# Asking for the first expert weights earlier and casting them later, in a fused attention and mixture-of-experts kernel

## The chip, the core and the metric

The kernel runs on one core of one Trainium2 chip. Five engines work side by side, each through its own list of instructions in order: TensorE (PE, with its weight loads as PEld), VectorE (DVE), ScalarE (ACT), GpSimd (POOL) and SyncE (SP), which here only issues transfers. They wait for each other through semaphores. The metric is the device time in microseconds (us), the median of several runs.

## The reference

```
a    = softmax(phi)                       # [8, 8, 576, 32], over the last axis
k_m  = a^T k ;  v_m = a^T v               # 32 memory slots for each batch and head
attn = softmax(q k_m^T / 8) ;  x = attn v_m   # -> 4608 tokens x 512
e    = argmax(x w_gate)                   # one expert of 8 for each token
gate = softmax(x w_gate)[e] * sigmoid(x w_output_gate)[e]
out  = gate * (relu(x w1[e]) w2[e])       # w1 512 x 1024, w2 1024 x 512
```

## The kernel before

**Two parts share the engines.** The attention goes through 20 groups, five for each of four pairs of batches. The memory part (`memory`) sums k and v into 32 slots per head; `scores`, `shift`, `expo`, `divide`, `back` and `values` make a group's attention; ACT copies the result out of PSUM (`xo`, line 902) and SP stores it to DRAM (`xs<-xo`, lines 1011 and 1015). After each pair `rank` and `route_early` or `route_late` sort its tokens by expert. The second part runs tokens of one expert through w1 and w2 in up to 36 slots; each slot gathers its tokens from `xs` (`xg`) and takes eight weight tiles of 512 KB (`w<-wall`, line 563).

**The order is written out by hand.** In each turn `t` the words of the list `ORDER` are gone through: S is `shift` of group t, X `expo` of group t-1, V0 and V1 the two halves of `values` of group t-3 with their copies, C `scores` of group t+1, M and m a step of the memory part, R a step of the routing, W the weights (`LAG` holds these distances). In turn 17 (`START`), after word S, the program opens: from there the slots' matmuls are the main stream, and three words of the attention are put in after each dozen or half dozen of them (`HOOK`). So what stands before the opening is attention alone, and what stands after it is matmuls of the experts with attention in between.

**Weights.** `Stream.fetch` issues loads while a raw buffer is free (three before the opening, two more after it, `raw`). `Stream.split` makes the pair of tiles `whl` that the matmuls use: ACT casts the raw tile to the rounded type (line 574) and DVE subtracts the cast from the raw tile (line 588). `take` and `done` call it, and word W calls it twice in turn 16, so that two tiles are ready at the opening. The loads of the first three tiles are issued by word W in turn 14.

**What can hold what.** SP issues transfers in the order of the program. The tile `xo` has two buffers, one for each turn: the copies of a turn wait until the store of the turn two before has landed. The tile `qt` has three; word C asks for the q of the group three ahead. `loads` asks for k and v in pairs of tiles, one pair for each step of `sums`. `pr` is one PSUM tile that the routing's small matmuls take in turn: `take_pr` waits in the program's order until the holder has issued its last read, `hold` lets a number of words pass, and only semaphores keep the next matmul from overtaking that read on the chip. After the opening the matmuls write `bps`, four PSUM banks in turn; the gathered tokens are first turned by PE (line 1086), then cast by ACT to `xh` (line 1088) and subtracted by DVE to `xl` (line 1089), then w1 follows (line 1238) and w2 (line 1275).

Of the kernel before, what the change touches and what calls it, by code (L numbers as in the profile page):

```python
# [18 lines left out]
B, H, S, D, M = 8, 8, 576, 64, 32  # L19
NTOK, DM, E, F = 4608, 512, 8, 1024  # L20
NBP = B // 2
# [13 lines left out]
NSLOT = NPE + NPT + NPP + NSS  # L35
NTHR = 13

ORDER = ["R4", "W", "X", "S", "R0", "m", "D", "M", "B", "V0", "R1", "R1", "V1", "M", "m", "C"]
LAG = {"X": 1, "B": 2, "D": 1, "V": 3, "C": -1}
TICK = 0  # L40
HOOK = (3, 2)
# [27 lines left out]
def attention_moe(tc, phiT, kv, qT, wgo, wall, out):  # L69
# [3 lines left out]
    with contextlib.ExitStack() as ctx:  # L73
# [206 lines left out]
        def route_early(k):  # L280
# [2 lines left out]
            eo, en = epcs[k], epcs[k + 1]  # L283
            yield from hold(LATE["ct"])
            yield from take_pr()
            n_ = counts(AFTER[k])
            yield
            yield from hold(LATE["dve"])
# [389 lines left out]
        def loads():  # L678

            load_phi(0)  # L680
            for bp in range(NBP):
                for c in (0, 2, 4, 6):
                    load_kv(bp, c)
                    load_kv(bp, c + 1)
                    if bp == 0 and c == 2:
                        load_kv(0, 8)
                        load_q(0)
                        load_q(1)
                    if bp == 0 and c == PHI1:
                        load_phi(1)  # L690
                    if bp == 0 and c == 6:
                        for n in range(2, NQ):
                            load_q(n)
                    yield

        def soften(bp):
# [414 lines left out]
        def attention():  # L1111

            nonlocal rou
            st, lgs = {}, {}
            while 0 not in kTs:
                mem.step()
            st[0] = scores(0, 0)
# [2 lines left out]
            for t in range(NT + LAG["V"]):  # L1120
                for w in ORDER:
                    g = t - LAG.get(w[0], 0)
                    if w in ("M", "m"):
                        if w == "M" or t % 5 < 4:
                            mem.step()
                    elif w[0] == "R":

                        if len(left) < NBP - 1:
                            rou.step(int(w[1:]) * (2 if len(left) == 1 else 1))
                    elif w == "W":  # L1130

                        if t == START - 3:
                            stream.fetch()
                        while t == START - 1 and stream.split(2):
                            pass
                    elif w == "V0" and 0 <= g < NT:
                        bp, c = g // 5, g % 5
                        while 2 * bp + (c >= 2) not in ves:
                            mem.step()
                        if g == 5 * bp:  # L1140
                            lgs[bp] = rt.tile([P, NCH, 16], F32, name="lg", bufs=2)
                        xo = wk.tile([P, 2, 2, 2 * XQ], F32, name="xo", bufs=2)
                        values(bp, 2 * c, st[g], xo)
                    elif w == "V1" and 0 <= g < NT:
                        if c < 4:
                            values(bp, 2 * c + 1, st[g], xo)
                        store(bp, c, xo, lgs[bp])
                    elif w == "C" and 0 < g < NT:
                        while 2 * (g // 5) + (g % 5 >= 2) not in kTs:
                            mem.step()  # L1150
                        st[g] = scores(g // 5, g % 5)
                        if g + NQ < NT:
                            load_q(g + NQ)
                    elif w == "S" and 0 <= g < NT:
                        shift(st[g])
                    elif w == "X" and 0 <= g < NT:
                        expo(st[g])
                    elif w == "D" and 0 <= g < NT:
                        divide(st[g])
                    elif w == "B" and 0 <= g < NT:  # L1160
                        back(st[g])
# [282 lines left out]
```

## Time and profile before

| | |
|---|---|
| runs | 553.48, 555.34, 555.79 us; median 555.34 |
| the profiled execution | 555.06 us, span 553.2 us |
| PE busy | 509.3 us, 92% of the span |
| ACT, DVE, POOL busy | 288.4, 351.1, 233.0 us |
| mean granted TensorE clock | 0.967 |
| first expert matmul (line 1238) | 119.32 us |
| transfers | 123.54 MB, mean 223 GB/s |

The profile is of one execution. Times count from the first instruction. The span is the time from the first to the last instruction; the run's own time has 1.9 us more around it. The granted clock is a share of full speed: 1.00 is 2.4 GHz and 0.50 is 1.2 GHz. "Idle before" names what ended an engine's idle time; where a wait is for several things, the profile puts it down to the one that came last, which is not always the one that held it.

### The profile page before, as it was taken

How to read it: one execution, taken by the hardware profiler on the slowest of the kernel's cores; microseconds unless marked ns; L12 is line 12 of the kernel's file. 1: busy time of each engine (PE TensorE's matmuls, PEld its weight loads, DVE VectorE, ACT ScalarE, POOL GpSimd, SP SyncE). 2: the span in 40 equal slices, each digit the busy share in tenths (PEclk: the TensorE clock that was granted, in tenths of full speed). 3: DMA queues.
4: the chain of work that ended last, by engine and by line, in shares of the span. 5: the costliest groups of instructions: out<-in, count | busy, mean ns of one | idle time of the engine just before them, and what ended most of it. 6: DMA issues, size and time to landing. Idle time of an engine off the chain costs nothing. (4 is left out here: it accounts for less than half of the span.)

```text
span 553.2 us, 10563 instructions
## 1 busy us (share of the span) xinstructions
PE 509.3 (92%) x3850; PEld 438.6 (79%) x3850; DVE 351.1 (63%) x779; ACT 288.4 (52%) x536; POOL 233.0 (42%) x254
## 2 busy tenths in 40 slices
PE   3778697779999999999999999999999999999993
PEld 2454465469689889898898989898999899988982
DVE  4274987677875649997555564954695387729310
ACT  3475565555345455643444554854685386548310
POOL 2242576750444223510376471745366453721101
PEclk9977978979999999999999999999999999999997
DMA  8999999995556846964456574776586578643001
GB/s 297 418 390 390 407 333 364 368 371 171 152 182 193 271 135 232 323 189 143 144 162 223 152 240 129 247 229 228 154 259 194 202 221 254 207 162 103 30 21 43
DMA packets 41998, 123.54 MB, mean 223 GB/s; under 512 B 10256, under 2 KB 10320, under 8 KB 41552
## 3 DMA queue, kind: packets, MB, share of 16 engines
q1 hardware_dynamic: 35136, 102.71, 56.3%
q0 software_dynamic: 6800, 20.06, 10.2%
q8 instruction: 32, 0.52, 0.4%
q14 instruction: 30, 0.25, 0.2%
HBM read 102.40 MB, written 20.35 MB: 222 GB/s over the span
## 5 line engine op out<-in xcount | busy, mean ns | idle before, releaser
L1275 PE MATMUL bps<-whl,hh 128*128 128x512 f32 x640 | 193.1, 394 | 0.0
L1238 PE MATMUL bps<-xh,whl 128*128 128x384 f32 x640 | 166.0, 336 | 0.7 <-DVE xl L1089 0.7
L588 DVE TENSOR_TENSOR whl<-w,whl 128x1024 fp32r<-128x1024 f32 x112 | 136.3, 1221 | 15.5 <-ACT whl L574 15.4
L1275 PEld LDWEIGHTS bps<-whl,hh 128*128 128x128 f32 x640 | 119.9, 188 | 24.6 <-issue 0.2
L574 ACT CAST whl<-w 128x1024 fp32r<-128x1024 f32 x112 | 116.6, 1045 | 22.1 <-PE bps L1275 16.3
L1238 PEld LDWEIGHTS bps<-xh,whl 128*128 128x128 f32 x640 | 115.8, 188 | 2.1 <-DVE xl L1089 0.9
L529 POOL DMA_INDIRECT xg<-xs,idx_ql x84 | 99.9, 1189 | 25.6 <-issue 23.5
L1238 PE MATMUL bps<-xl,whl 128*128 128x384 f32 x320 | 107.0, 334 | 0.0
L1275 PE MATMUL bps<-whl,hl 128*128 128x512 f32 x240 | 93.7, 390 | 0.0
L1243 DVE SCALAR_TENSOR_TENSOR hl<-bps,hh 128x384 fp32r<-128x384 f32 x80 | 44.0, 555 | 61.4 <-ACT hh L1242 61.4
L1242 ACT ACTIVATE hh<-bps 128x384 fp32r<-128x384 f32 x80 | 38.9, 492 | 77.7 <-PE bps L1238 77.6
L1211 POOL DMA_INDIRECT out<-y,idx_ol x23 | 24.9, 1084 | 108.7 <-ACT y L1210 52.4
L1238 PEld LDWEIGHTS bps<-xl,whl 128*128 128x128 f32 x320 | 60.1, 188 | 0.3
L1275 PEld LDWEIGHTS bps<-whl,hl 128*128 128x128 f32 x240 | 45.1, 188 | 8.5
L869 POOL TENSOR_TENSOR ea<-ea,mx 128x512 f32<-128x512 f32 (+1 forms) x20 | 19.2, 962 | 50.4 <-DVE mx L867 46.0
L1233 PE MATMUL bps<-xh,whl 128*128 128x384 f32 x128 | 37.7, 338 | 0.0
L1234 PE MATMUL bps<-xh,whl 128*128 128x256 f32 x128 | 35.7, 279 | 0.0
L902 ACT COPY xo<-bpd 128x576 f32<-128x576 f32 x36 | 22.7, 639 | 22.6 <-issue 9.0
L1210 ACT ACTIVATE y<-bps,gx 128x512 f32<-128x512 f32 x19 | 13.1, 688 | 40.1 <-PE bps L1275 28.6
L1211 POOL DMA_INDIRECT out<-y,idx_ob x9 | 9.8, 1087 | 49.4 <-ACT y L1210 37.4
L900 PE MATMUL bpd<-ve_b,aT 64*128 64x144 f32 (+1 forms) x320 | 29.0, 333 | 0.7 <-DVE ea L863 0.5
L863 DVE STREAM_TRANSPOSE ea<-bpd 128x512 f32<-128x512 f32 (+1 forms) x20 | 13.2, 659 | 25.0 <-PE bpd L853 25.0
(263 smaller groups left out, 599.0 us busy)
## 6 DMA issues: line engine op xcount, KB each, us to landing
w<-wall SPq DMA_DIRECT2D x112, 512.0 KB, 4.6
kvt<-kv SPq DMA_DIRECT2D x32, 512.0 KB, 8.3
xs<-xo SPq DMA_DIRECT2D x16, 576.0 KB, 5.8
qt<-qT SPq DMA_DIRECT2D x16, 512.0 KB, 9.3
ph<-phiT SPq DMA_DIRECT2D x3, 1152.0 KB, 11.9
kv<-kv SPq DMA_DIRECT2D x4, 512.0 KB, 9.2
xg<-xs,idx_ql POOLq DMA_INDIRECT x84, 4.5
ph<-phiT SPq DMA_DIRECT2D x4, 288.0 KB, 3.8
```

The costliest lines, as they stand in the source:

```text
L529: G.indirect_dma_start(out=z["xg"][:, k, XQ * b:XQ * b + XQ], out_offset=None, in_=xs[0:z["rows"]].rearrange("t (a q) -> (t a) q", a=4), i ...
L574: A.copy(hl[:, 0], w[:])
L588: V.tensor_tensor(hl[:, 1], w[:], hl[:, 0].bitcast(F32), ALU.subtract)
L900: T.matmul(px[to:to + n, r, sl], z["aT"][h, o:o + n], ves[2 * bp + b][h, g], start=True, stop=True)
L902: A.copy(xo[:, c % 2], px[:, :, 0:2 * XQ])
L1211: G.indirect_dma_start(out=out, out_offset=bass.IndirectOffsetOnAxis(ap=z["idx"][1][0:n, z["q0"] + k:z["q0"] + k + 1], axis=0), in_=y[0:n] ...
L1233: T.matmul(pb, w[:, 0, o:o + P], x[0][:, cc], start=(cc == 0), stop=False)
L1234: T.matmul(pb[:, 0:256], w[:, 1, o:o + P], x[0][:, cc, 0:256], start=False, stop=(cc == 3))
L1238: T.matmul(pb, w[:, b, o:o + P], x[a][:, cc, 0:n_], start=(n == 0), stop=(n == 11))
L1242: A.activation(h_[:, j], pb, AF.Relu)
L1243: V.scalar_tensor_tensor(l_[:, j], pb, 0.0, h_[:, j].bitcast(F32), ALU.max, ALU.subtract)
L1275: T.matmul(py[k], a, w[:, b, DM * f:DM * f + DM], start=(u == 4 and f == 0 and n == 0), stop=(u == 7 and f == 1 and n == len(ps) - 1))
```

## The change

It has three parts. The first three weight loads leave word W of turn 14 and go into `loads`, right behind the last k and v; word W moves from ahead of X to behind V1, so that the two casts of turn 16 stand behind the copies of that turn. The q of groups 18 and 19 is no longer asked for by word C of turns 14 and 15, but by word X of turn 17, just ahead of the opening. The second call of `route_early` lets three more words pass before its count matmul (line 277).

```diff
-ORDER = ["R4", "W", "X", "S", "R0", "m", "D", "M", "B", "V0", "R1", "R1", "V1", "M", "m", "C"]
+ORDER = ["R4", "X", "S", "R0", "m", "D", "M", "B", "V0", "R1", "R1", "V1", "W", "M", "m", "C"]
...
             yield from take_pr()
+            if k:
+                yield from hold(LATE["pe"])
             n_ = counts(AFTER[k])
...
                         for n in range(2, NQ):
                             load_q(n)
+                    if (bp, c) == (NBP - 1, 6):
+                        stream.fetch()
                     yield
...
-            st, lgs = {}, {}
+            st, lgs, held = {}, {}, []
...
                     elif w == "W":
 
-                        if t == START - 3:
-                            stream.fetch()
                         while t == START - 1 and stream.split(2):
                             pass
...
-                        if g + NQ < NT:
+                        if START < g + NQ < NT:
+                            held.append(g + NQ)
+                        elif g + NQ < NT:
                             load_q(g + NQ)
...
                     elif w == "X" and 0 <= g < NT:
+                        while t == START and held:
+                            load_q(held.pop(0))
                         expo(st[g])
```

**SP's queue, from the last k and v to the opening.** `w` are weights, `kvt` k and v, `qt` q, `xo` the copies of the attention's result and `gt` the gates of a pair. The stores of turns 13 to 16 are those of `xo_1526`, `xo_1628`, `xo_1729`, `xo_1805` before, and `xo_1541`, `xo_1628`, `xo_1727`, `xo_1791` now. Before:

```order
L675 DMA kvt_1515<-kv 128x1024
L675 DMA kvt_1517<-kv 128x1024
L1011 DMA xs_60<-xo_1526 128x2x576
L670 DMA qt_1582<-qT 128x1024
...
L563 DMA w_1610<-wall 128x1024
...
L563 DMA w_1612<-wall 128x1024
...
L563 DMA w_1614<-wall 128x1024
L1011 DMA xs_60<-xo_1628 128x2x576
L670 DMA qt_1681<-qT 128x1024
```

and now:

```order
L677 DMA kvt_1515<-kv 128x1024
L677 DMA kvt_1517<-kv 128x1024
...
L565 DMA w_1528<-wall 128x1024
...
L565 DMA w_1530<-wall 128x1024
...
L565 DMA w_1532<-wall 128x1024
L1015 DMA xs_60<-xo_1541 128x2x576
L672 DMA qt_1597<-qT 128x1024
L1015 DMA xs_60<-xo_1628 128x2x576
```

Three weights now stand ahead of the store of turn 13 and of the q of group 17. Further down, the fourth and fifth weight come behind the store of turn 16, and the two late q behind these.

**ACT, the last instructions ahead of the opening,** with what each waits for (`DMAHW` are semaphores of SP's transfers). `xo_1729` before and `xo_1727` now are the copies of turn 15. Before:

```order
L902 COPY xo_1729<-bpd_1730 128x576 [waits DMAHW5_49,DVE_49,PE_49]
L902 COPY xo_1729<-bpd_1736 128x576 [waits PE_49]
L574 CAST whl_1771<-w_1610 128x1024 [waits DMAHW7_49]
L574 CAST whl_1776<-w_1612 128x1024 [waits DMAHW0_49]
L873 ACTIVATE ea0_203<-ea0_203 128x16x32 [waits Pool_49]
L779 ACTIVATE kvm_1787<-pk_1647,rs_1338 128x128 [waits PE_49]
...
L902 COPY xo_1805<-bpd_1806 128x576 [waits DMAHW2_49,DVE_49,PE_49]
L902 COPY xo_1805<-bpd_1812 128x576 [waits PE_49]
L873 ACTIVATE ea1_204<-ea1_204 128x16x32 [waits Pool_49]
L1088 CAST xh_1876<-bps_1878 128x384 [waits PE_49]
```

and now:

```order
L906 COPY xo_1727<-bpd_1728 128x576 [waits DMAHW0_49,DVE_49,PE_49]
L906 COPY xo_1727<-bpd_1734 128x576 [waits PE_49]
L877 ACTIVATE ea0_203<-ea0_203 128x16x32 [waits Pool_49]
L783 ACTIVATE kvm_1773<-pk_1647,rs_1338 128x128 [waits PE_49]
...
L906 COPY xo_1791<-bpd_1792 128x576 [waits DMAHW2_49,DVE_49,PE_49]
L906 COPY xo_1791<-bpd_1798 128x576 [waits PE_49]
L576 CAST whl_1805<-w_1528 128x1024 [waits DMAHW5_49]
L576 CAST whl_1810<-w_1530 128x1024 [waits DMAHW6_49]
L877 ACTIVATE ea1_204<-ea1_204 128x16x32 [waits Pool_49]
L1092 CAST xh_1876<-bps_1878 128x384 [waits PE_49]
```

The two casts move from behind the copies of turn 15 to behind those of turn 16. DVE's two subtractions move with them: they now stand directly ahead of these rows, which before followed on turn 16's own work:

```order
L590 TENSOR_TENSOR whl_1805<-w_1528,whl_1805 128x1024 [waits DMAHW5_49,Activation_49]
L590 TENSOR_TENSOR whl_1810<-w_1530,whl_1810 128x1024 [waits DMAHW6_49,Activation_49]
L811 COPY ve_b_1774<-bpa_1815 128x2x16 [waits PE_49]
L867 STREAM_TRANSPOSE ea2_205<-bpd_1825 128x16x32 [waits DVE_49,PE_49]
L871 TENSOR_REDUCE mx_1850<-ea2_205 128x16 [waits DVE_49]
L1023 TENSOR_REDUCE lg_1540<-xo_1791 128x32
L1093 TENSOR_TENSOR xl_1877<-bps_1878,xh_1876 128x384 [waits Activation_49]
```

**PE, the count matmul of the second `route_early`** (line 277 in both). Before:

```order
L1086 MATMUL bps<-ident,xg 128x128 x3
L1275 MATMUL bps<-whl,hh 128x512
L1275 MATMUL bps<-whl,hl 128x512
L1275 MATMUL bps<-whl,hh 128x512 x2
L1275 MATMUL bps<-whl,hl 128x512
L1275 MATMUL bps<-whl,hh 128x512
L277 LDWEIGHTS ones_b
L277 MATMUL pr<-ohc_91,ones_b 128x8
```

and now:

```order
L1090 MATMUL bps<-ident,xg 128x128 x3
L1281 MATMUL bps<-whl,hh 128x512
L1281 MATMUL bps<-whl,hl 128x512
L1281 MATMUL bps<-whl,hh 128x512 x2
L1281 MATMUL bps<-whl,hl 128x512
L1281 MATMUL bps<-whl,hh 128x512 x2
L1281 MATMUL bps<-whl,hl 128x512
L1281 MATMUL bps<-whl,hh 128x512 x2
L1281 MATMUL bps<-whl,hl 128x512
L1281 MATMUL bps<-whl,hh 128x512
L277 LDWEIGHTS ones_b
L277 MATMUL pr<-ohc_91,ones_b 128x8
```

Six matmuls of 512 columns more stand ahead of it.

## Rows read from the trace of the kernel before

**Rows 1.** Who waited for whom on PE from 118 us to the end: engine, line, what it waited for; us in total, times, longest us. These are all rows of the answer.

```profile
PE pr L277 <- DVE w__2038 L963: 1.0, 1, 1.0
PE bps L1238 <- DVE xl L1089: 0.7, 1, 0.7
```

**Rows 2.** The timeline of PE around the opening: start us, us, engine, line, operation, tiles, count, and in brackets the idle time before and what ended it.

```profile
104.40 1.25 PE L900 MATMUL bpd<-ve_b,aT 64*128 64x144 f32 x16
...
107.65 0.67 PE L853 MATMUL bpd<-qt,kT 64*32 64x256 f32 x16 [0.78 <-ACT xo L902]
112.79 0.74 PE L788 MATMUL bpa<-ident,kvm 128*128 128x128 f32 x2 [4.47 <-ACT kvm L779]
113.45 2.29 PE L900 MATMUL bpd<-ve_b,aT 64*128 64x144 f32 x16
...
116.90 1.77 PE L1086 MATMUL bps<-ident,xg 128*128 128x128 f32 x12
119.32 0.45 PE L1238 MATMUL bps<-xh,whl 128*128 128x384 f32 x1 [0.65 <-DVE xl L1089]
...
128.74 0.66 PE L853 MATMUL bpd<-qt,kT 64*32 64x256 f32 x16
```

**Rows 3.** The timeline of ACT around the opening, columns as in Rows 2.

```profile
106.96 1.18 ACT L902 COPY xo<-bpd 128x576 f32<-128x576 f32 x2 [3.19 <-PE pk L768]
109.39 1.04 ACT L574 CAST whl<-w 128x1024 fp32r<-128x1024 f32 x1 [1.25 <-DMA w<-wall]
110.90 1.04 ACT L574 CAST whl<-w 128x1024 fp32r<-128x1024 f32 x1 [0.47 <-DMA w<-wall]
111.85 0.63 ACT L873 ACTIVATE ea<-ea 128x512 f32<-128x512 f32 x1
112.38 0.61 ACT L779 ACTIVATE kvm<-pk,rs 128x128 f32<-128x128 f32 x2
...
115.79 0.64 ACT L902 COPY xo<-bpd 128x576 f32<-128x576 f32 x1 [0.32 <-PE bpd L900]
116.33 0.63 ACT L873 ACTIVATE ea<-ea 128x512 f32<-128x512 f32 x1
```

**Rows 4.** The timeline of SP's queue ahead of the opening (start us, us of issuing, line, transfer, count). The row at 106.88 is the second store of `gt`, which waits for the store of the row at 97.58 to land.

```profile
97.58 0.38 SPq L1011 DMA_DIRECT2D xs<-xo  x1
...
100.16 1.68 SPq L563 DMA_DIRECT2D w<-wall  x3
...
106.88 0.96 SPq L983 DMA_DIRECT2D xs<-gt  x1
108.11 0.38 SPq L980 DMA_DIRECT2D xs<-gt  x1
...
113.73 1.64 SPq L563 DMA_DIRECT2D w<-wall  x2
```

**Rows 5.** What SP's queue waited for from 80 to 130 us: us in total, times, longest us.

```profile
SPq L983 <- DMA xs<-xo: 1.0, 1, 1.0
SPq L983 <- DMA w<-wall: 0.9, 1, 0.9
```

**Rows 6.** The timeline of POOL: the subtraction of group 15's row maximum, which `expo` in turn 16 waits for.

```profile
108.32 1.04 POOL L869 TENSOR_TENSOR ea<-ea,mx 128x512 f32<-128x512 f32 x1
```

**Rows 7.** The timeline of DVE around the opening, columns as in Rows 2.

```profile
110.47 1.23 DVE L588 TENSOR_TENSOR whl<-w,whl 128x1024 fp32r<-128x1024 f32 x1 [3.76 <-ACT whl L574]
...
116.16 0.19 DVE L807 COPY ve_b<-bpa 128x32 f32<-128x32 f32 x1
117.08 0.72 DVE L863 STREAM_TRANSPOSE ea<-bpd 128x512 f32<-128x512 f32 x1 [0.74 <-PE bpd L853]
...
118.72 1.94 DVE L1089 TENSOR_TENSOR xl<-bps,xh 128x384 fp32r<-128x384 f32 x4
...
125.27 2.36 DVE L588 TENSOR_TENSOR whl<-w,whl 128x1024 fp32r<-128x1024 f32 x2 [0.38 <-ACT whl L574]
```

**Rows 8.** The timeline of PE around the count matmul of the second `route_early`.

```profile
144.71 0.40 PE L1275 MATMUL bps<-whl,hh 128*128 128x512 f32 x1
146.10 0.18 PE L277 MATMUL pr<-ohc,ones_b 128*128 128x8 bf16 x1 [1.00 <-DVE w__2038 L963]
146.15 0.48 PE L1275 MATMUL bps<-whl,hh 128*128 128x512 f32 x1
...
147.39 0.62 PE L1275 MATMUL bps<-whl,hh 128*128 128x512 f32 x2
```

**Rows 9.** The timeline of DVE: the last read of `pr` ahead of that matmul.

```profile
145.83 0.22 DVE L963 TENSOR_TENSOR w__2038<-ohg,pr 128x72 f32<-128x72 bf16 x1
```

**Rows 10.** The timeline of PE: two more places in the attention where PE had stood still.

```profile
63.80 0.17 PE L277 MATMUL pr<-ohc,ones_b 128*128 128x8 bf16 x1 [2.03 <-DVE ohc L944]
...
85.72 0.59 PE L788 MATMUL bpa<-ident,kvm 128*128 128x128 f32 x2 [3.05 <-ACT kvm L779]
```

**Rows 11.** Stretches of time: length, busy us and instructions of PE, PEld, DVE, ACT, POOL; then the granted clock, the DMA engines' busy share and GB/s.

```profile
64.00:65.00 1.00, 1.00 (x28) 0.83 (x30) 0.96 (x2) 0.51 (x1) 0.00 (x0) 1.00 1.04 402
...
87.00:88.00 1.00, 1.00 (x10) 0.75 (x8) 0.00 (x0) 0.90 (x2) 0.88 (x1) 0.50 1.05 422
...
117.00:117.50 0.50, 0.50 (x3) 0.50 (x4) 0.41 (x1) 0.00 (x0) 0.32 (x1) 0.57 1.08 340
```

**Rows 12.** The page's list of transfers: count, KB each, median us from issue to landing.

```profile
qt<-qT SPq DMA_DIRECT2D x16, 512.0 KB, 9.3
```

## The prediction

> **What bounds the kernel now.** I read first who waits for whom on PE from 118 us on. The answer has two rows [rows 1]: 1.0 us ahead of one routing matmul and 0.7 us ahead of the first expert matmul, and nothing else for 430 us. So from 119.32 us, where the first expert matmul starts [rows 2], the kernel is bound by PE, and the end moves with two things alone: the time of that first matmul, and whatever makes PE stand still or run slowly behind it. Work of ACT, DVE, POOL or SP behind 119 us costs nothing as long as PE does not wait for it.
>
> Next come the timelines of PE, ACT, DVE and SP ahead of the opening, to see what the first expert matmul waits for. PE stands still for 4.47 us up to 112.79, waiting for `kvm` of ACT [rows 2]. ACT reaches `kvm` late because the two weight casts stand ahead of it: they start at 109.39 and 110.90, each the moment its weight has landed, then `expo` at 111.85 and `kvm` at 112.38 [rows 3]. Behind that comes a chain: `kvm`, its turning on PE, the copies of turn 16 on ACT (the second at 115.79, [rows 3]), scores of group 17, DVE's transpose of them at 117.08, then `xl` at 118.72 [rows 7] and the first expert matmul 0.60 us later.
>
> One more row matters, and the profile names the wrong releaser for it. The copies of turn 15 start at 106.96 after 3.19 us of idle time "<-PE pk" [rows 3]. Their own matmuls started at 104.40, and all 16 took 1.25 us [rows 2], so PE did not hold them. They also wait for the store of turn 13, and SP's queue shows when it landed: its next transfer waited for `xs<-xo` and went out at 106.88 [rows 4, 5]. That store was issued at 97.58 [rows 4], so it was under way for 9.3 us. It is the store that released ACT, 0.08 us later.
>
> **The change, part by part.**
>
> *The weights move ahead of that store.* Three weights of 512 KB now stand in SP's queue between the last k and v and the store of turn 13. Transfers of this queue land one behind the other: the store at 106.88, the q at 108.11 (SP's next issue), the first weight at 109.39, the second at 110.90 [rows 3, 4]; SP's own waits name the store and the weight [rows 5]. That is 1.23, 1.28 and 1.51 us for one, so three weights put the store back by 3.7 to 4.5 us. I take 4.0: copies of turn 15 at 111.0 instead of 106.96. From below the bound is 0, if the transfers' rate leaves room for the weights; nothing in the queue shows such room, so I stay near the upper end.
>
> The Trainium skill, "DMA: Bandwidth & Descriptors", section "Queues, rings and completion order", says that each DMA engine consumes descriptors in ring order; the spaced landings agree. The same section says that completion is nevertheless not first-in, first-out for one issuing engine; by that the store could land near 106.9 all the same, which is the first rival below.
>
> *The casts leave the place ahead of `expo`.* Alone this would give much back: `expo` would wait only for POOL, which ends at 109.36 [rows 6], and `kvm` would stand 0.53 us behind it (111.85 to 112.38, [rows 3]) at 109.9, 2.45 us earlier. With the copies at 111.0 it is otherwise: they take 1.18 us less an overlap of 0.1, `expo` starts at 112.05 and `kvm` at 112.6. That is 0.2 us later than before. The wait for the weights is replaced by a wait for a store that stands behind the weights.
>
> *The casts come in behind the copies of turn 16.* From `kvm` to the second copy 3.41 us pass as before (112.38 to 115.79), so it starts at 116.0; 0.54 us on (115.79 to 116.33, [rows 3]) the first cast, at 116.55. The first subtraction starts 1.08 us behind its cast (109.39 to 110.47, [rows 3, 7]), at 117.63; a pair takes 2.36 us [rows 7] and ends at 120.0. In the order the copy of `ve_b` (0.19 us, mostly overlapped) and the transpose of group 17's scores stand behind it, and these did not wait for any weight before. From that transpose 1.64 us to `xl` (117.08 to 118.72, [rows 7]) and 0.60 us to the first expert matmul [rows 2, 7]: 122.2 instead of 119.32. **Term: +2.9 us.** PE's turning of the gathered tokens also waits for the `ve_b` copy; it runs beside DVE's transpose and adds nothing. The bounds: with the store landing as before the same chain starts at 109.9 and ends at 119.6, +0.3; with 4.5 us for the weights, +3.4. If PE ran at full clock here, 16 matmuls of `values` would take 1.25 instead of 2.29 us [rows 2], 1.04 less.
>
> *The count matmul.* It waits 1.00 us for a DVE read that starts at 145.83 and takes 0.22 [rows 8, 9]. It now has six more matmuls ahead of it. Five take 1.24 us (146.15 to 147.39, [rows 8]), so the six end about 1.4 us behind 145.1, when the read is over. **Term: -1.0 us**, between 0 and -1.0.
>
> *The clock.* Ahead of the opening, PE finishes scores of group 17 at about 117.1 (116.90 before, [rows 2], plus 0.2) and then has nothing until the `ve_b` copy at 120.0: a gap of 2.9 us right in front of the PE-bound stretch, where before it was 0.65. After a gap of 3.05 us the clock was at 0.50, that is 1.2 GHz, from 87 us; after one of 2.03 it stayed at 1.00 [rows 10, 11]. The gap here is nearest to the first. What a low clock takes: in the last low stretch PE worked from 112.79 [rows 2] until the clock came back within 117.0 to 117.5 [rows 11], 4.6 us. At half speed that loses 2.3 us of expert matmuls if all of it falls on them, 0 if the clock holds. The turning of the tokens comes first and takes some of it; I take the middle. **Term: +1.1 us.**
>
> The Trainium skill, "TensorE: Matmul & The Clock Gate", section "What's actually happening", speaks against this change too: the throttled state is the default there and activity releases it, so a gap moved to the front of dense work is paid by that work. Here that is the term just given.
>
> *At nothing.* The late q: SP reaches it behind two weights that wait for the subtractions (120.0) and 1.64 us of issuing [rows 4], so at about 121.5; it lands 9.3 us later [rows 12], at 130.8. Its scores stood 9.4 us behind the first expert matmul [rows 2] and stand a dozen matmuls, some 2 us, later now: 133.7. The cover is 2.9 us. The q of group 17 lands behind the store at about 112.3 and is used at 116. The fourth and fifth weights are asked for after the subtractions, as before, and are cast after the first expert results. The later routing steps shift by one or two places among matmuls, where PE waited for none of them [rows 1].
>
> *The sum:* +2.9 - 1.0 + 1.1 = +3.0 on the profiled execution's 555.06 us: **558.1 us**. That execution stands 0.3 us under the median of the runs, 555.34; I leave the difference out.
>
> **The rivals.**
>
> 1. *The store is not held.* If it lands near 106.9 in spite of the weights, the first expert matmul comes at 119.6 (+0.3), or at 118.5 (-0.8) if the shorter gap ahead of `kvm`, 2.0 instead of 4.47 us, leaves the clock up. With -1.0 for the count matmul and 0 to +1.1 for the clock: -1.8 to +0.4, around **554.4 us**, not slower than before. It decides if the three weights cost the store less than about 1 us. For it: the weights were issued at 100.16 [rows 4] and can now go out some 2 us earlier. Against it: the landings one by one [rows 4, 5].
> 2. *The store is held, the clock is not.* The clock is at 1.00 both in the chain and at the first expert matmuls: +2.9 - 1.04 - 1.0 = +0.9, **556.0 us**. For it: the clock stayed up after 2.03 us [rows 10, 11]. Against it: PE would now be idle from about 107 to 111.7, longer than the 4.47 us after which `values` took 2.29 us [rows 2].
> 3. *The late q holds PE as well.* Scores of group 18 stand between expert matmuls, so every microsecond by which the q misses its 2.9 us of cover stops PE. With 2 us missed: **560.1 us**. Against it: fewer transfers are under way by then.
>
> **How the numbers follow.** The forecast has a chance of 0.62, rival 1 of 0.20, rival 2 of 0.11, rival 3 of 0.07. A measurement of this kernel can tell about 0.5%, 2.8 us, from no change: faster is below 552.6, slower above 558.1. The forecast lies on that line, and half of its chance goes to either side; with rival 3 slower has 0.40. Rivals 1 and 2 are no change but for the lowest end of rival 1 with the scatter of the runs: faster 0.07. No change keeps 0.53. The range: the forecast's own from 556.5 (clock held at the first matmuls) to 559.8 (+3.4 and all 2.3 of the clock, less 1.0), down into rival 1 and up towards rival 3: 554.0 to 560.2.
>
> **What would show it.** Right: copies of turn 15 near 111 with idle time ahead of them, `kvm` near 112.6, the subtractions up to about 120, the first expert matmul near 122, the granted clock at 0.50 for one or two microseconds behind it, no wait at line 277. Wrong: copies of turn 15 at 107, or the first expert matmul at or before 119.5. A wait of PE for q or for a weight behind the opening would be rival 3.

## The result and the profile after

| | before | after |
|---|---|---|
| median of 8 runs each, in turn on one chip | 555.16 us (552.65 to 556.64) | 557.66 us (556.80 to 560.20) |
| ratio | | 1.0054, 95% interval 1.003 to 1.0077 |
| the profiled execution | 555.06 us, span 553.2 | 556.8 us, span 555.1 |
| mean granted clock | 0.967 | 0.962 |

The change costs 2.5 us by the medians, 0.5%: the forecast was 558.1. Of some kernels a few executions take over 1.5% longer than the fastest one; the ratios leave these out, and two profiled executions below, that of the weights behind the store (563.53 us) and that of the changed kernel once more (570.34 us), are of that kind. The change acts in the 25 us ahead of the first expert matmul, and there one has to know where each execution stands: these two differ by about 1 us before the changed part begins. So I count from one row that is the same in both programs, the second copy of `xo` in turn 13 on ACT, and write such times with a plus.

That row in the timeline of ACT of the kernel before (start us, us, engine, line, operation, tiles, count):

```profile
96.93 0.63 ACT L902 COPY xo<-bpd 128x576 f32<-128x576 f32 x1
```

And ACT of the kernel after; the last bracket of a row is the idle time ahead of it and what ended it:

```profile
95.89 0.63 ACT L906 COPY xo<-bpd 128x576 f32<-128x576 f32 x1
...
109.80 1.18 ACT L906 COPY xo<-bpd 128x576 f32<-128x576 f32 x2 [7.07 <-DMA xs<-xo]
...
111.39 0.63 ACT L783 ACTIVATE kvm<-pk,rs 128x128 f32<-128x128 f32 x2
...
114.82 0.64 ACT L906 COPY xo<-bpd 128x576 f32<-128x576 f32 x1 [0.32 <-PE bpd L904]
115.35 1.99 ACT L576 CAST whl<-w 128x1024 fp32r<-128x1024 f32 x2
```

The copies of turn 15 stood at +10.0 (106.96, [rows 3]) and now stand at +13.9. This time the profile names what holds them: the store `xs<-xo`, 7.07 us long. `kvm` has lost the two casts ahead of it and stands where it stood all the same: +15.5 in both. The casts come behind the second copy of turn 16.

SP's queue ahead of the opening (start us, us of issuing, line, transfer, count):

```profile
97.41 1.62 SPq L565 DMA_DIRECT2D w<-wall  x3
99.14 0.38 SPq L1015 DMA_DIRECT2D xs<-xo  x1
...
117.69 1.49 SPq L565 DMA_DIRECT2D w<-wall  x2
119.28 0.84 SPq L672 DMA_DIRECT2D qt<-qT  x2
```

The store of turn 13 stands behind the three weights. In the kernel before it was issued at +0.65 and landed 9.3 us later [rows 4]. Now SP issues the weights first, so it is issued at +3.25 (99.14), and it is 10.7 us under way (to 109.80). The two parts, 2.6 us and 1.3 us, say where the time shows and not what costs it, for the DMA engines were at work all along. From the counted row to the copies of turn 15, in the kernel before and then in the kernel after (stretch and length; busy us and instructions of PE, PEld, DVE, ACT, POOL; granted clock, DMA share, GB/s):

```profile
96.93:106.96 10.03, 9.06 (x207) 6.25 (x199) 9.35 (x30) 4.93 (x13) 7.14 (x12) 1.00 0.99 354
...
95.89:109.80 13.91, 9.31 (x207) 6.42 (x199) 9.33 (x30) 4.93 (x14) 10.09 (x15) 1.00 1.02 394
```

Their mean share is 0.99 and 1.02. By an estimate from the last row three weights of 512 KB at 394 GB/s take 4.0 us, as much as the whole delay of 3.9 us. An earlier issue of the store in the same order was not tried.

DVE and PE, columns as for ACT:

```profile
116.43 2.36 DVE L590 TENSOR_TENSOR whl<-w,whl 128x1024 fp32r<-128x1024 f32 x2 [1.82 <-ACT whl L576]
118.71 0.18 DVE L811 COPY ve_b<-bpa 128x32 f32<-128x32 f32 x1
118.81 0.71 DVE L867 STREAM_TRANSPOSE ea<-bpd 128x512 f32<-128x512 f32 x1
```

```profile
110.49 1.11 PE L857 MATMUL bpd<-qt,kT 64*32 64x256 f32 x16 [4.40 <-ACT xo L906]
...
118.95 2.82 PE L1090 MATMUL bps<-ident,xg 128*128 128x128 f32 x12 [2.96 <-DVE ve_b L811]
121.42 0.67 PE L1244 MATMUL bps<-xh,whl 128*128 128x384 f32 x1
```

The copy of `ve_b` and the transpose of group 17 now stand behind the subtractions, and PE waits 2.96 us for the first of the two, ahead of turning the gathered tokens and of the expert matmuls behind that. The first of these starts at +25.5 where it started at +22.4 (119.32, [rows 2]). It takes 0.67 us instead of 0.45: PE is at half speed. No idle time stands between the turning and it, so it was the turning, at half speed, that ended last. Stretches of time, columns as for the DMA engines above:

```profile
110.00:110.50 0.50, 0.01 (x2) 0.01 (x3) 0.00 (x0) 0.50 (x2) 0.00 (x0) 0.77 1.22 256
...
123.50:124.00 0.50, 0.50 (x3) 0.50 (x3) 0.00 (x0) 0.00 (x0) 0.48 (x1) 0.58 0.92 283
```

Between these rows the clock is at 0.50 throughout, 13.6 us. It falls during the wait for the copies of turn 15, not in the gap that I had named, and it is still low for the first 2.5 us of expert matmuls, which loses half of them, 1.25 us.

Who waited for whom on PE from 118 us on, the whole answer:

```profile
PE bps L1090 <- DVE ve_b L811: 3.0, 1, 3.0
```

The 1.0 us at line 277 [rows 1] is gone, and PE waits neither for q nor for a weight. The sum of what is seen: +3.1 for the opening, +1.25 for the clock, -1.0 for line 277, -1.04 because this execution came to turn 13 earlier: +2.3, and the span is 1.9 us longer; 0.4 us are not accounted for.

### The profile page after: what moved, and what is told of

Its sections match the earlier page's. It is cut to its first block, busy times and chain, and to the rows that moved or that the text cites. A ratio compares the mean times of both kernels' runs of the same rounds, so it can differ in the third digit from the quotient of the medians.

```text
span 555.1 us, 10562 instructions
## 1 busy us (share of the span) xinstructions
PE 511.5 (92%) x3850; PEld 440.8 (79%) x3850; DVE 350.7 (63%) x779; ACT 287.8 (52%) x536; POOL 236.6 (43%) x254
## 5 line engine op out<-in xcount | busy, mean ns | idle before, releaser
L590 DVE TENSOR_TENSOR whl<-w,whl 128x1024 fp32r<-128x1024 f32 x112 | 136.0, 1219 | 13.8 <-ACT whl L576 13.8
L1281 PEld LDWEIGHTS bps<-whl,hh 128*128 128x128 f32 x640 | 119.9, 188 | 24.6 <-issue 0.2
L576 ACT CAST whl<-w 128x1024 fp32r<-128x1024 f32 x112 | 116.5, 1045 | 16.0 <-PE bps L1281 13.6
L531 POOL DMA_INDIRECT xg<-xs,idx_ql x84 | 102.4, 1218 | 25.6 <-issue 23.2
L1217 POOL DMA_INDIRECT out<-y,idx_ol x23 | 25.1, 1093 | 107.6 <-ACT y L1216 52.4
L906 ACT COPY xo<-bpd 128x576 f32<-128x576 f32 x36 | 22.6, 638 | 25.4 <-PE bpd L904 9.2
L867 DVE STREAM_TRANSPOSE ea<-bpd 128x512 f32<-128x512 f32 (+1 forms) x20 | 13.2, 659 | 30.3 <-PE bpd L857 30.2
L1217 POOL DMA_INDIRECT out<-y,idx_ob x9 | 10.7, 1184 | 46.2 <-ACT y L1216 37.2
```

The source lines that it names most:

```text
L531: G.indirect_dma_start(out=z["xg"][:, k, XQ * b:XQ * b + XQ], out_offset=None, in_=xs[0:z["rows"]].rearrange("t (a q) -> (t a) q", a=4), i ...
L576: A.copy(hl[:, 0], w[:])
L590: V.tensor_tensor(hl[:, 1], w[:], hl[:, 0].bitcast(F32), ALU.subtract)
L906: A.copy(xo[:, c % 2], px[:, :, 0:2 * XQ])
L1217: G.indirect_dma_start(out=out, out_offset=bass.IndirectOffsetOnAxis(ap=z["idx"][1][0:n, z["q0"] + k:z["q0"] + k + 1], axis=0), in_=y[0:n] ...
L1281: T.matmul(py[k], a, w[:, b, DM * f:DM * f + DM], start=(u == 4 and f == 0 and n == 0), stop=(u == 7 and f == 1 and n == len(ps) - 1))
```

## The experiments

**Theory A** is that of the prediction: the store of turn 13 is held behind the weights, the late casts stand in the chain to the opening, and the gap this leaves on PE is paid at low clock. **Theory B** is that one of these is not so; what it says instead stands in each expectation. The runs of one kernel scattered over 3 to 13 us here, so a ratio resolves 0.3 to 0.6%, and I rest on the timelines. Each timeline is of one execution. In the kernels that have the order of the kernel before up to the copies of turn 15 (before, fetch in turn 14, hold only, and the kernel before with 34 filler matmuls) these stand at +8.9 to +10.6, so differences of about a microsecond there are scatter. Times with a plus count from the second copy of turn 13, as above.

| run | copies turn 15 | `kvm` | first expert matmul | from `kvm` to it | ratio, 95% interval |
|---|---|---|---|---|---|
| before | +10.0 | +15.5 | +22.4 | 6.9 | |
| after | +13.9 | +15.5 | +25.5 | 10.0 | 1.0054 (1.003 to 1.0077) |
| fetch in turn 14 | +10.6 | +12.6 | +24.8 | 12.2 | 1.0120 (1.0062 to 1.0177) |
| hold only | +10.5 | +15.7 | +22.6 | 6.9 | 1.0002 (0.9950 to 1.0055) |
| casts early | +14.0 | +17.5 | +24.5 | 7.0 | 1.0062 (1.0020 to 1.0105) |
| behind the store | +10.8 | +14.7 | +21.7 | 6.9 | 1.0012 (0.9971 to 1.0054) |
| changed again | +15.1 | +16.7 | +26.6 | 9.8 | 1.0059 (1.0020 to 1.0098) |
| 12 filler matmuls | +14.0 | +15.6 | +25.3 | 9.6 | 1.0004 (0.9962 to 1.0047) |
| three `xo` | +8.3 | +13.2 | +23.2 | 10.0 | 1.0012 (0.9969 to 1.0055) |
| three `xo`, casts early | +8.3 | +13.9 | +20.9 | 6.9 | 0.9984 (0.9951 to 1.0017) |
| the same again | +7.9 | +13.8 | +20.6 | 6.8 | 0.9951 (0.9922 to 0.9981) |
| the same, 30 filler matmuls | +7.9 | +13.5 | +21.9 | 8.4 | 0.9997 (0.9960 to 1.0034) |
| before, hold, 34 filler matmuls | +8.9 | +14.0 | +22.9 | 8.9 | 0.9979 (0.9949 to 1.0009) |
| no hold | +13.5 | +15.1 | +25.1 | 10.0 | one execution, 565.34 us |

### The fetch back in turn 14

```diff
 # against the kernel after
-                    if (bp, c) == (NBP - 1, 6):
-                        stream.fetch()
...
                     elif w == "X" and 0 <= g < NT:
+                        if t == START - 3:
+                            stream.fetch()
```

> The changed kernel with one part undone: the first three weights are asked for where the kernel before asked for them, behind the store of turn 13 and the q of group 17; late casts, late q and the later count matmul stay. Theory A (the store of turn 13, held up behind the weights, holds the copies of turn 15): the copies start 0.1 us behind the landing of that store, some 2.9 us earlier than in the changed kernel when counted from turn 13's copy, and the first expert matmul comes some 2.5 us earlier; the clock is still low for about 1 us of expert matmuls, so 555.2 to 556.0 us, 2 us less than the changed kernel. Theory B (the casts and subtractions ahead of the opening cost it, wherever the weights stand): the first expert matmul stays within 0.7 us of the changed kernel's 121.4, and so does the time, 557 to 558.

ACT, then PE, of this kernel:

```profile
97.49 0.63 ACT L904 COPY xo<-bpd 128x576 f32<-128x576 f32 x1
...
108.11 1.18 ACT L904 COPY xo<-bpd 128x576 f32<-128x576 f32 x2 [4.16 <-PE pk L770]
...
115.12 1.18 ACT L904 COPY xo<-bpd 128x576 f32<-128x576 f32 x2 [3.07 <-DMA xs<-xo]
```

```profile
122.27 0.56 PE L1244 MATMUL bps<-xh,whl 128*128 128x384 f32 x1
```

The first half came as Theory A has it: with the weights out of the way the copies of turn 15 are back at +10.6 and `kvm` comes 2.9 us earlier than in the kernel after. The second half failed: the opening gains 0.7 us only. The store of turn 14 stands behind the same weights, and the copies of turn 16 wait 3.07 us for it, up to +17.6. It stood behind them in the kernel before too, but there nobody waited for it. It was issued at 102.46 and was 11.1 us under way, so it landed at +16.6, and ACT came to the copies of turn 16 only at +17.9 (SP's queue, then ACT, of the kernel before):

```profile
102.46 0.38 SPq L1011 DMA_DIRECT2D xs<-xo  x1
...
114.83 0.64 ACT L902 COPY xo<-bpd 128x576 f32<-128x576 f32 x1 [0.35 <-PE bpd L900]
```

The wait was moved to the next store. The ratio, with six runs, is worse than the timeline accounts for; why is open.

### The hold alone

```diff
 # against the kernel before
             yield from take_pr()
+            if k:
+                yield from hold(LATE["pe"])
```

> The kernel before with the third part alone: the second route_early lets three words pass ahead of its count matmul. Theory A: the wait of 1.0 us at line 277 is gone, the opening is that of the kernel before, and the time falls by 1.0 us, to 554.2. Theory B: the wait only moves to another small matmul of the routing, and the time stays.

PE's waits from 118 us on, the whole answer:

```profile
PE bps L1277 <- issue: 2.5, 3, 1.1
PE bps L1240 <- issue: 0.4, 1, 0.4
```

No wait at line 277 and the opening at +22.6, as before. The gain of 1.0 us is there in the waits; the ratio is too wide to show it. The two rows "<- issue" are time in which PE waited for nothing that the profile shows. They total 2.9 us here, and neither kernel has them in its own profile.

### The casts back in their old place

```diff
 # against the kernel after
-ORDER = ["R4", "X", "S", "R0", "m", "D", "M", "B", "V0", "R1", "R1", "V1", "W", "M", "m", "C"]
+ORDER = ["R4", "W", "X", "S", "R0", "m", "D", "M", "B", "V0", "R1", "R1", "V1", "M", "m", "C"]
```

> The changed kernel with another part undone: the two casts stand behind the copies of turn 15 again, as before; the weights stay ahead of the store of turn 13. Theory A: the copies of turn 15 start as late as in the changed kernel, about 109.8 (some 3 us later than before); the casts no longer wait for weights, so kvm comes about 2 us behind them and the first expert matmul near 121, but PE's gap right ahead of it shrinks to under 1 us and the clock is full there: 556.4 us. Theory B (the place of the casts is what costs): as the kernel before, 555.2 less 1.0 for line 277, 554.2.

```profile
97.82 0.63 ACT L906 COPY xo<-bpd 128x576 f32<-128x576 f32 x1
...
111.84 1.18 ACT L906 COPY xo<-bpd 128x576 f32<-128x576 f32 x2 [7.18 <-DMA xs<-xo]
112.91 2.00 ACT L576 CAST whl<-w 128x1024 fp32r<-128x1024 f32 x2
...
115.33 0.63 ACT L783 ACTIVATE kvm<-pk,rs 128x128 f32<-128x128 f32 x2
```

```profile
122.29 0.44 PE L1244 MATMUL bps<-xh,whl 128*128 128x384 f32 x1 [0.29 <-DVE xl L1093]
```

This takes the change's two delays apart. The copies of turn 15 are at +14.0, held as in the kernel after: that is the fetch's doing. The casts cost 2.0 us ahead of `kvm` (+17.5 instead of +15.5) and no longer 3.1 us behind it (7.0 us to the opening instead of 10.0). No gap is left ahead of the opening, and the first expert matmul takes 0.44 us, full clock. So of the 3.1 us of the opening, 2.1 are the early fetch: the copies come 4.0 us later, and 2.0 of that come back because the casts no longer wait for weights. The late casts add 1.0, and the low clock behind the opening.

### Weights right behind the store of turn 13

```diff
 # against the kernel before; has the hold of the count matmul too
-                        if t == START - 3:
-                            stream.fetch()
...
+                        if t == START - 4:
+                            stream.fetch()
```

> The kernel before with the later count matmul, and with the first three weights asked for right behind the store of turn 13, ahead of the q of group 17; casts and late q as before. Theory A: the store is not held up, copies of turn 15 as before (106.9 less the scatter of the start), the weights land one q transfer earlier, 1.3 to 1.5 us, so kvm and the first expert matmul come 1.3 to 1.5 us earlier; with 1.0 us at line 277, 552.6 us, faster than both. Theory B (something else than the weights' landing holds the casts): only the 1.0 us, 554.2.

```profile
96.23 0.63 ACT L904 COPY xo<-bpd 128x576 f32<-128x576 f32 x1
...
107.06 1.18 ACT L904 COPY xo<-bpd 128x576 f32<-128x576 f32 x2 [3.98 <-DMA xs<-xo]
108.22 1.04 ACT L576 CAST whl<-w 128x1024 fp32r<-128x1024 f32 x1
109.48 1.04 ACT L576 CAST whl<-w 128x1024 fp32r<-128x1024 f32 x1 [0.22 <-DMA w<-wall]
```

The fetch now stands behind `store` and ahead of the q of group 17. One place further back in SP's queue, and the store is not held: copies at +10.8. The first cast no longer waits for its weight, the second waits 0.22 us, where the two waited 1.25 and 0.47 us before [rows 3]. That is 1.5 us less, as expected, but the copies ahead of them stood 0.8 us later in this execution, so the opening is 0.7 us earlier than before. The ratio does not tell this from no change.

### The changed kernel once more

The kernel after, unchanged, on the chip of the next three.

> The changed kernel once more, on the chip of the next three, as their base: 2.5 us above the kernel before; counted from the second copy of turn 13, copies of turn 15 at +13.9, kvm at +15.5, first expert matmul at +25.5 (before: +10.0, +15.5, +22.4).

Ratio 1.0059, as in the first comparison. In its profiled execution, of 570.34 us, the copies of turn 15 were held to +15.1 and the first expert matmul came at +26.6, 1.1 to 1.2 us later than expected, with a gap of 3.46 us on PE ahead of the turning. It repeats the order of events.

### Filler matmuls in the gap ahead of the opening

```diff
 # against the kernel after, ahead of the turning of the tokens; nothing reads the result
+        fill = ps_k.tile([P, 2, 2 * D], F32, name="pk")
+        for _ in range(12):
+            T.matmul(fill[:, 0], ident[:], ident[:], start=True, stop=True)
```

> The changed kernel with twelve idle-time matmuls (the identity times itself, into a PSUM tile that nothing reads) right ahead of the turning of the gathered tokens, where PE waits 3 us for DVE. Theory A (PE's gap ahead of the opening is what leaves the clock low for the first expert matmuls): the clock is at 1.00 from the first expert matmul on; the turning takes under 1.8 instead of 2.8 us, and the time falls by 1.0 to 1.5 us against the changed kernel. Theory B (the low clock comes from the earlier standstill, of 4.4 us up to scores of group 16, and lasts whatever PE does): the clock stays at 0.50 up to the same place and the time stays.

```profile
116.06 3.58 PE L1400 MATMUL pk<-ident 128*128 128x128 f32 x24
119.48 1.47 PE L1090 MATMUL bps<-ident,xg 128*128 128x128 f32 x12
121.17 0.44 PE L1244 MATMUL bps<-xh,whl 128*128 128x384 f32 x1 [0.22 <-DVE xl L1093]
```

```profile
117.00:117.50 0.50, 0.50 (x5) 0.50 (x4) 0.50 (x1) 0.50 (x2) 0.00 (x0) 0.57 0.98 369
```

With PE kept at work the clock comes back at 117.4 and stays: the turning takes 1.47 us instead of 2.82, the first expert matmul 0.44 instead of 0.67. The opening itself is where it was (+25.3), since DVE's chain sets it: PE waits 0.22 us for `xl` here. So Theory A's clock term holds: with the gap filled the 1.25 us of expert matmuls are not lost. The other runs agree. In all five with 2.9 to 3.5 us of idle time on PE ahead of the turning (after, fetch in turn 14, changed again, three `xo`, no hold) the first expert matmul starts at 0.50; in the nine others, the kernel before among them, it starts at 1.00. The ratio, 1.0004 against 1.0059 of the changed kernel on the same chip, goes the same way, but the two intervals overlap from 1.0020 to 1.0047.

### Three buffers for `xo`

```diff
 # against the kernel after; room from one raw weight buffer less and two merged small tiles
-NRAW = 3
+NRAW = 2
...
-GROW = ((2, 2, 2), (6, 1, 0))
+GROW = ((2, 3, 2), (6, 1, 0))
...
-                        xo = wk.tile([P, 2, 2, 2 * XQ], F32, name="xo", bufs=2)
+                        xo = wk.tile([P, 2, 2, 2 * XQ], F32, name="xo", bufs=3)
```

> The changed kernel with a third buffer for the copies, so that those of turn 15 wait for the store of turn 12 and those of turn 16 for that of turn 13; to make room, two weights instead of three are asked for early, and three raw buffers instead of two come at the opening. Theory A (the held store is what delays the opening): copies of turn 15 start about +8.5 us from turn 13's, right behind their matmuls; then expo waits for POOL only, kvm comes at +13, the first expert matmul at +22.8, 2.7 us earlier than in the changed kernel, and the time falls by 2 to 3 us. Theory B (the casts' new place alone): the first expert matmul stays at +25 or later.

```profile
105.57 1.18 ACT L906 COPY xo<-bpd 128x576 f32<-128x576 f32 x2 [1.48 <-issue]
```

```profile
117.99 2.82 PE L1089 MATMUL bps<-ident,xg 128*128 128x128 f32 x12 [3.21 <-DVE ve_b L811]
120.46 0.67 PE L1243 MATMUL bps<-xh,whl 128*128 128x384 f32 x1
```

The edit also has two weights ahead of the store instead of three. Nothing of the store is waited for any more, and the copies of turn 15 come at +8.3. That takes the first delay away and leaves the second: from `kvm` to the opening still 10.0 us, with the gap (3.21 us) and the low clock.

### Three buffers for `xo`, and the casts early

```diff
 # against the kernel of the run above: the order of the kernel before
-ORDER = ["R4", "X", "S", "R0", "m", "D", "M", "B", "V0", "R1", "R1", "V1", "W", "M", "m", "C"]
+ORDER = ["R4", "W", "X", "S", "R0", "m", "D", "M", "B", "V0", "R1", "R1", "V1", "M", "m", "C"]
```

> The same with the casts behind the copies of turn 15 again. Theory A: copies of turn 15 at +8.5, the casts right behind them or when the weights land, at about +10 and +11, kvm at +13, and nothing of the casts between the copies of turn 16 and the opening: first expert matmul at +20, 2.4 us earlier than in the kernel before, clock full there; with the count matmul 3.4 us below the kernel before, faster than both. Theory B: the store of turn 13 now holds the copies of turn 16 instead, and the first expert matmul stays at +22 or later.

> The same kernel once more (three xo buffers, early casts), beside the version with the 30 matmuls on the same chip. Timeline as in its first run: copies of turn 15 about 8.3 us, kvm 13.9, first expert matmul 20.9 us behind the second xo copy of turn 13. By the opening (1.5 us earlier than in the kernel before) and line 277 (1.0) it should be 2.5 us faster than before, ratio 0.9955; its first ratio was 0.9984 with 0.9951 to 1.0017. If it is 0.998 or more again, something of these 2.5 us is given back behind the opening.

The second time, ACT and PE:

```profile
98.43 0.63 ACT L906 COPY xo<-bpd 128x576 f32<-128x576 f32 x1
...
106.33 1.21 ACT L906 COPY xo<-bpd 128x576 f32<-128x576 f32 x2 [1.48 <-issue]
...
111.67 0.63 ACT L877 ACTIVATE ea<-ea 128x512 f32<-128x512 f32 x1 [1.04 <-POOL ea L873]
```

```profile
118.99 0.45 PE L1243 MATMUL bps<-xh,whl 128*128 128x384 f32 x1 [0.90 <-DVE xl L1092]
```

With both delays gone the opening comes at +20.9 and +20.6, 1.5 to 1.8 us earlier than in the kernel before, at full clock. I had expected +20; the missing part is a wait of `expo` for POOL ahead of `kvm`, about 1 us. The first time the ratio did not tell this from no change; the second time it is 0.9951 (0.9922 to 0.9981), 2.7 us by 557.52, against 2.5 expected. So this version is faster than the changed kernel (1.0059, 1.0020 to 1.0098, on the chip of its first run), and by the second run alone 0.5% faster than the kernel before. What the third buffer would give in the kernel before, without the early fetch, was not run.

### Filler matmuls in the wait for `kvm`

```diff
 # against the kernel of the run above (34 of them in the kernel before with the hold); overwritten
+                if bp == NBP - 1 and b == 1:
+                    for _ in range(30):
+                        T.matmul(pt[:, 0], ident[:], ident[:], start=True, stop=True)
                 for g in range(2):
                     T.transpose(pt[:, g], z[b]["kv"][:, g], ident[:])
```

> The version with three xo buffers and early casts, and on PE 30 matmuls of the identity with itself ahead of the last turning of kvm (line 794), whose result is overwritten: about 3.7 us at 0.12 us each (1.47 us for 12 of such size at full clock in the run with 12 of them), in a gap that was 3.82 us long. Theory A (the gap costs through the clock): clock 1.00 from there on, the 16 matmuls of values in about 1.25 us instead of 2.29, turning of the tokens about 1.5 us instead of 2.5, first expert matmul about 19.6 us behind the second xo copy of turn 13 instead of 20.9; 1 to 2 us less than without the 30 matmuls, and some 3 to 4 us less than the kernel before (ratio 0.993 to 0.996). Theory B (the clock falls whatever PE does here, or the chain of ACT and DVE hides PE's slowness): clock at 0.50 as before, or clock up but the first expert matmul no earlier than 20.6; ratio as without them.

> The kernel before with the wait at line 277 taken out by holding the count matmuls, and 34 matmuls of the identity with itself ahead of the last turning of kvm: about 4.1 us in a gap of 4.47. Nothing of the fetches or casts is changed. Theory A: clock 1.00 through the opening, values in about 1.25 us instead of 2.29, first expert matmul about 21.4 us behind the second xo copy of turn 13 instead of 22.4 to 22.6; with the 1.0 us of line 277 some 2 us less than the kernel before (ratio 0.996). Theory B: clock at 0.50 as before, first expert matmul at 22.4 or later; ratio 0.998 to 1.000.

PE of the first of the two:

```profile
107.45 6.96 PE L793 MATMUL bpa<-ident 128*128 128x128 f32 x60
...
114.56 1.25 PE L907 MATMUL bpd<-ve_b,aT 64*128 64x144 f32 x16
...
119.31 0.45 PE L1246 MATMUL bps<-xh,whl 128*128 128x384 f32 x1 [0.87 <-DVE xl L1095]
```

Half of Theory A: the clock was at 1.00 in every stretch from 108 us on, and `values` took 1.25 us instead of 2.29. But I had mis-sized the filling. Such a matmul shows as two instructions (60 for 30, and 24 for 12 in the run above, which I had overlooked), so it took 6.96 us in a gap of 3.9 and itself held the turning of `kvm` back. The opening came at +21.9, later than without it. In the kernel before the same happened (7.9 us, opening +22.9). What a filling of the right length would give was not tried.

### The change without the hold

```diff
 # against the kernel after
-            if k:
-                yield from hold(LATE["pe"])
```

> The changed kernel without the hold of the count matmuls: only this part of the change is undone. Its place for the count matmul is that of the kernel before. Theory A (the hold alone takes the wait away): PE waits about 1.0 us at line 277 again, opening as in the changed kernel, first expert matmul 25 to 26 us behind the second xo copy of turn 13. Theory B (the later opening alone would have taken the wait away): no wait at line 277.

PE's waits from 118 us on:

```profile
PE bps L1279 <- issue: 3.9, 8, 1.0
PE bps L1088 <- DVE ve_b L809: 3.5, 1, 3.5
PE pr L277 <- DVE w__2038 L965: 1.0, 1, 1.0
```

The wait at line 277 is back at its full 1.0 us although the opening is late. So the hold alone takes it away.

## Why the prediction was right

**The opening, +2.9: right, measured +3.1.** The steps, counted from turn 13: copies of turn 15 forecast at +14.1, came at +13.9; `kvm` +15.7, came +15.5; second copy of turn 16 +19.1, came +18.9; first expert matmul +25.3, came +25.5. That the store is held, and by the weights, is shown from both sides: ahead of it they hold it (+13.5 to +14.0 in three other kernels), one place behind it they don't (+10.8). The size was right too, 3.9 us for 4.0. Landings one behind the other are borne out by the DMA engines, whose mean share over that time was 1.02: at their 394 GB/s three weights take 4.0 us. One step was wrong by a little. I wrote that the turning of the tokens adds nothing to the chain; at half speed it took 2.82 us and set the first expert matmul, 0.25 us later than with the 12 filler matmuls (+25.3).

**The casts: right.** Behind the copies of turn 16 they cost 3.1 us between `kvm` and the opening (10.0 against 6.9); ahead of `kvm` 2.0.

**The count matmul, -1.0: right.** The wait is gone with the hold (in the kernel before and after alike) and back without it. In the times of the runs it is too small to see.

**The clock, +1.1: right in size, with the wrong beginning.** I expected the clock to fall in the gap of 2.9 us ahead of the opening. The gap was 2.96 us, but the clock had fallen at 110.3, in the wait for the copies of turn 15, and had not come back. The gap kept it down, as the 12 filler matmuls show. The Trainium skill, "TensorE: Matmul & The Clock Gate", section "What's actually happening", says that activity releases the low state. The fillers agree with that (clock back at 117.4); the matmuls from 110.49 to 115.99 in the kernel after did not release it. 1.25 us were lost; with it the sum of the terms is +3.35 us, inside the interval of the ratio (1.7 to 4.3 us).

That 1.25 came so near to the middle that I had taken is luck. The loss is half of the time from the first expert matmul to the return of the clock, and by that the fetch in turn 14 lost 0.15 us and the kernel with three `xo` 0.4 us with the same gap; two longer executions lost 1.6 us (changed again, 570.34 us) and 1.7 us (no hold, 565.34 us). The ends of the low stretch in the first two, with first expert matmuls at 122.27 and 120.46:

```profile
122.50:123.00 0.50, 0.50 (x4) 0.50 (x4) 0.48 (x1) 0.35 (x1) 0.50 (x1) 0.94 0.80 287
...
121.00:121.50 0.50, 0.50 (x4) 0.50 (x3) 0.42 (x2) 0.33 (x1) 0.50 (x1) 0.78 1.35 279
```

The rows that I had for it were too few as well. The wait of 2.03 us after which the clock stayed up [rows 10, 11] was followed by one of 2.10 us, and then it fell, at 69.6 us in the kernel before:

```profile
68.26 0.19 PE L953 MATMUL pr<-ohg,strict 128*128 128x72 bf16 x1 [2.10 <-DVE tge L191]
```

```profile
69.50:70.00 0.50, 0.50 (x17) 0.18 (x9) 0.50 (x9) 0.50 (x1) 0.00 (x0) 0.65 1.02 418
```

**The range.** By its terms the forecast's own lower end, with nothing for the clock, is 557.0 and not 556.5; the range stated went down to 554.0 for rival 1, so nothing hangs on it.

**The rivals.** Rival 1, the store not held, fell by the rows of ACT and SP. What it would have given, 554.4 us, may have been too simple as well: in the first experiment the store of turn 13 is free, and the store of turn 14 holds the copies of turn 16. I had looked at one store where two stand behind the weights. The Trainium skill, "DMA: Bandwidth & Descriptors", section "Queues, rings and completion order", says that completion is not first-in, first-out for one issuing engine; for these large transfers the traces show the order of the queue deciding (+13.9 behind the weights, +10.8 ahead of them). Rival 2 fell with the clock at 0.50, rival 3 with no wait of PE for q: the two late q were issued at 119.28, +23.4, where I had them at +24.6. No run undid the late q alone; that it costs nothing is read from PE's waits.

**What stays open.** Set beside what opening, clock and line 277 add up to, the times of the experiments stand 0.5 to 2.4 us higher in six of the ten runs that this can be worked out for, 0.7 and 1.7 us lower in two, and about 5 us higher for the fetch in turn 14. The intervals of the ratios are 1.7 to 3.2 us wide to either side, so only the last stands clearly outside. Their profiles of PE have 0.6 to 6.5 us of "<- issue" inside the expert matmuls there, which the two profiles of before and after do not have. There is no profile of the kernel before from those chips, so whether it had the same is not known.

## What to carry to other kernels

Ahead of moving a fetch to an earlier place in a queue, list every transfer that it now stands in front of, and who waits for the landing of each: here two stores set free the buffers of the next copies. The fetch cost 2.1 us of the opening ahead of the first of them, gained 0.7 us behind it, and 1.5 to 1.8 us once the copies had a buffer more. Work that is taken from ahead of one step lands ahead of another: the casts cost less in front of `kvm` than behind the copies, where they opened a gap on PE right ahead of dense matmuls. A wait that the profile puts down to an engine which had long been done is worth a look at the queue.

## What the runs showed that I had not expected

- The same wait of PE can leave one low stretch or two. In the kernel after the clock stayed at 0.50 from 110.3 to 123.9, through the matmuls from 110.49 to 115.99; in the run with three `xo` it fell at 111.0, was at 1.00 again from 114.4 to 117.8 and fell in the gap. The changed kernel once more, the same program, also had two stretches (111.3 to 118.1 and 121.5 to 128.4).
- Executions came to the second copy of turn 13 at 95.5 to 98.6 us, with hardly a difference in the instructions before it. Stages that wait for transfers must be compared from a common row, not from the start.
- The wait for the store is named "<-PE pk" in some profiles ([rows 3], and the run with the fetch back in turn 14) and "<-DMA xs<-xo" in others, for the same two rows of the program.
